# Batch 1 loaded and transposed like batch 0, and GpSimd making the integer addition for w_in's words

## The chip, the cores and the metric

One core of a Trainium2 chip runs the kernel: TensorE (PE, matrix products), VectorE (DVE), ScalarE (ACT), GpSimd (POOL), and SyncE (SP), from whose queue all DMAs of this kernel are issued. The metric is the device time of one execution in microseconds (us), as the median of several runs.

## The reference

Two stages. First, for 8 batches of 8 heads with 576 tokens of 64 dimensions, 32 packed queries p attend to k and v, and the tokens' queries q then attend to the packed result:

```python
def sm_attn(qq, kk, vv):
    s = scale * np.matmul(qq, kk.transpose(0, 1, 3, 2))
    s = s - np.max(s, axis=-1, keepdims=True)
    a = np.exp(s)
    a = a / (np.sum(a, axis=-1, keepdims=True) + 1e-09)
    return np.matmul(a, vv)
p_packed = sm_attn(p, k, v)
out = sm_attn(q, p_packed, p_packed)
```

Its 4608 rows of 512 go through a feed-forward layer with w_in (512 x 2048) and w_out (2048 x 512):

```python
h = x @ w_in
h2 = h * h
h3 = h2 * h
P = a[0] + a[1] * h + a[2] * h2 + a[3] * h3
Q = 1.0 + np.abs(b[0]) * np.abs(h) + np.abs(b[1]) * h2
g = P / (Q + 1e-06)
return (g @ w_out).astype(np.float32)
```

w_in and w_out come in as float64, 8.4 MB each, and the kernel makes float32 of them itself.

## The kernel before, in words

**Units.** The work is cut into 128 units: 8 batches, 2 halves x of 288 tokens, 8 chunks c of 256 hidden columns. `hidden` computes a unit's h in PSUM and the rational function (tiles U, V, Y), and splits the result into a high and a low part, gh and gl. `acc_block` multiplies these by w_out's parts (wh, wl) three units later and accumulates in `acc`. The last 64 tokens of each batch are kept in G and treated two batches at a time by `remainder`.

**Folding.** h is not x @ w_in: `m_chunk(bb, c)` forms M from the packed values (PPT) and w_in, in the PSUM banks `at`, and `hidden` multiplies M by the weights of the second attention, which `attention(bb)` leaves transposed in AH and AL (high and low part).

**Attention.** `attention(bb)` is a generator of 16 steps, laid between the units of the batch before; batch 1's steps lie among batch 0's units. Its steps: k transposed (`transposed("k", g)`), p transposed, scores and exponentials, their transposes, the product with v, q transposed, the second scores, the second softmax. Batch 0 runs ahead of all units and takes another route than the others:
- Batch 0 (`bb == 0`): k, q and v are loaded in long rows, 512 KB in one DMA; PE transposes k and q block by block into PSUM banks and ACT copies them to KX. The last 64 tokens of k and q are loaded apart into a tile r (in a buffer of Y), and transposed by PE as well. The keys lie in parts of 256 and 320, each with a maximum of its own, and a few small DVE operations join the two.
- Batches 1 to 7 (`bb > 0`): k and q are loaded in 144 KB pieces of 128-byte rows so that DVE's 32x32 transpose brings them straight from `nat` into KX; the keys lie in two halves of 288 with a common maximum.

`bank(bb)` gives batch 0 the banks of both `acc` and `at`, and later batches those of `at` alone (2 banks).

**Conversion of the words.** `load_words` brings raw float64 words into buffers that are free at that time (those of m, w, o); `convert` makes float32 of one chunk: two ACT operations (the high word rescaled, the low word's top bits to an integer di), a DVE mask for the sign, a DVE shift-and-or, and the integer addition of hi and di. For w_in (8 chunks, kind "in") the addition writes `win`; for w_out (kind "out") it is followed by a split into high and low part by ACT and POOL. The 17 conversions run from before the first unit into the tenth.

**Order.** All operations are recorded first. `Planner` then ranks them by its own table of costs per engine and writes out the order on every engine, the DMAs on SP's queue too; tiles that share a buffer (`Ring`) follow one another in the order of the program. Each engine works through its list in order. Since every call goes out through one helper, all instructions carry line L216 in the profile, and tiles tell them apart.

Of the kernel before, what the change touches and what calls it, by code (L numbers as in the profile page):

```python
# [13 lines left out]
F32 = mybir.dt.float32  # L14
# [9 lines left out]
P = 128  # L24
# [223 lines left out]
def attention_rational_ffn(  # L248
# [140 lines left out]
    def convert():  # L389
        nonlocal converted  # L390
        if converted == len(words):
            return
        load_words(AHEAD)
        (kind, i, n), raw = words[converted], words_in[converted][1]
        x = 4 if kind == "in" else n
        w = raw.bitcast(I32).rearrange("p (x y two) -> p x y two", x=x, two=2)
        lo, hi = w[:, :, :, 0], w[:, :, :, 1]

        if kind == "in":
            dst = win[:, i // 2]  # L400
            di = dst.bitcast(I32)
        else:
            dst = lo.bitcast(F32)
            di = w_ring.at(i // 2, [P, n * DM], I32) if n == 2 else full_ring.next(dtype=I32)
            di = di.rearrange("p (x y) -> p x y", x=n)
        nc.scalar.activation(hi.bitcast(F32), hi.bitcast(F32), AF.Copy, scale=REBIAS)

        nc.scalar.activation(di, lo.bitcast(U32), AF.Copy, scale=2.0**-29)
        nc.vector.tensor_scalar(lo, hi, -0x80000000, None, ALU.bitwise_and)
        nc.vector.scalar_tensor_tensor(hi, hi, 3, lo, ALU.logical_shift_left, ALU.bitwise_or)  # L410
        nc.vector.tensor_add(dst.bitcast(I32), hi, di)
        if kind == "out":
            if i // 2 not in W:
                W[i // 2] = w_ring.at(i // 2)
            for y in range(n):
                split(dst[:, y, :], *(W[i // 2][:, (i + y) % 2, x, :] for x in range(2)))
        converted += 1
        load_words(AHEAD)
# [6 lines left out]

    NAT, AH, AL, PPT = {}, {}, {}, {}

    def load(bb, what):  # L430
        if bb >= B:
            return
        if what == "rem":

            rv, pn = NAT[bb, "rv"], NAT[bb, "p"] = rv_ring.next(), pn_ring.next()
            if bb == 0:
                r = NAT[bb, "r"] = Y_ring.at(2, [P, H, D])
                nc.sync.dma_start(r[0:REM], k[bb, :, NS * P : T, :].rearrange("h p d -> p h d"))
            for j in range(NJ):
                src = p[bb, NG * j : NG * j + NG].rearrange("r n d -> n r d")  # L440
                nc.sync.dma_start(pn[32 * j : 32 * j + 32, :, 0, :], src)
            nc.gpsimd.tensor_copy(pn[:, :, 1, :], pn[:, :, 0, :])
            for i in range(2 if bb == 0 else 0):
                src = q[bb, 4 * i : 4 * i + 4, NS * P : T, :].rearrange("h (p x) d -> p h (x d)", x=2)
                r2 = r[REM + HREM * i : REM + HREM * (i + 1)].rearrange("p (h x) d -> p h (x d)", x=2)
                nc.sync.dma_start(r2, src)
            for i in range(2):
                src = v[bb, 4 * i : 4 * i + 4, NS * P : T, :]
                if bb == 0:
                    nc.sync.dma_start(rv[REM * i : REM * (i + 1)], src.rearrange("h p d -> p h d"))  # L450
                    continue
                for y in range(2):
                    o = REM * i + HREM * y
                    nc.sync.dma_start(rv[o : o + HREM], src.rearrange("h (p y) d -> y p h d", y=2)[y])
            return
        x, g = what[0], int(what[1])
        src = {"k": k, "q": q, "v": v}[x][bb, 4 * g : 4 * g + 4]
        if bb > 0:
            t = NAT[bb, what] = nat_ring.next()
            if x == "v":  # L460
                t = NAT[bb, what] = t[:, 0 : 4 * NS * D].rearrange("p (h s d) -> p h s d", h=4, s=NS)
                for y in range(2):
                    to = t.rearrange("p h (y i) d -> p h y (i d)", y=2)[:, :, y]
                    nc.sync.dma_start(to, src[:, 2 * P * y : 2 * P * (y + 1)].rearrange("h (p i) d -> p h (i d)", i=2))
                return
            src = src.rearrange("h t d -> (h t) d")
            for i in range(2):
                for y in range(2):
                    o = 64 * i + 32 * y
                    blocks = src[:, 32 * y : 32 * y + 32].rearrange("(a t i) d -> i t a d", t=32, i=2)[i]  # L470
                    nc.sync.dma_start(t[o : o + 32].rearrange("p (a d) -> p a d", d=32), blocks)
            return
        src = src[:, 0 : NS * P, :]
        if x != "k":
            if g == 0:
                NAT[x] = w_ring.at(NCH - 2 + "vq".index(x), [P, 2, 4 * NS * D], F32)
            t = NAT[x][:, g, :]
        else:
            t = nat_ring.next()[:, 0 : 4 * NS * D]
        t = t.rearrange("p (h s d) -> p h s d", h=4, s=NS)  # L480
        nc.sync.dma_start(t, src.rearrange("h (p s) d -> p h s d", s=NS))
        NAT[bb, what] = t
# [18 lines left out]
    def attention(bb):  # L501
# [7 lines left out]
        xr = lambda x: x.rearrange("p (x r) -> p x r", r=NG)  # L509
        eng = nc.vector if bb == 0 else nc.gpsimd  # L510
        KX = kx_ring.next()
        AH[bb], AL[bb], PPT[bb] = AH_ring.next(), AL_ring.next(), ppT_ring.next()
        flat = KX.rearrange("p j c -> p (j c)")
        rows = lambda i: slice(64 * i, 64 * i + 64)
        cols = lambda j: slice(32 * j, 32 * j + 32)
# [4 lines left out]
        qx = flat.rearrange("p (r j c) -> p r j c", r=NG, j=NJ)  # L520

        def transposed(x, g):
            for r in range(NG if bb > 0 else 0):

                src = NAT[bb, f"{x}{g}"].rearrange("p (j r c) -> p r j c", j=2, r=NG)[:, r]
                nc.vector.transpose(qx[:, r, 2 * g : 2 * g + 2, :], src)
            for r in range(NG if bb == 0 else 0):
                t = bank(bb)
                for i in range(2):
                    for y in range(2):  # L530
                        o = (2 * i + y) * P
                        nc.tensor.transpose(t[:, o : o + P], NAT[bb, f"{x}{g}"][:, 2 * i + r, 2 * y : 2 * y + 2, :], ident)
                to = kmain if x == "k" else qx[:, :, :, 0:HMAIN]
                nc.scalar.copy(to[:, r, 2 * g : 2 * g + 2, :], t.rearrange("p (j c) -> p j c", j=2))
# [4 lines left out]
                load(bb, f"v{g}")  # L539
            yield  # L540
        rkq = NAT.get((bb, "r"))
        if bb == 0:
            t = bank(bb)
            for j in range(NJ):
                nc.tensor.transpose(t[:, j * P : (j + 1) * P], rkq[:, 2 * j : 2 * j + 2, :], ident)
            nc.scalar.copy(krem, t.rearrange("p (j c) -> p j c", j=NJ)[:, :, 0:REM])
# [3 lines left out]
        nc.scalar.copy(pT, t[:, 0 : NG * P].rearrange("p (r c) -> p r c", r=NG))  # L550
        yield

        KEYS = ((0, 2 * P), (2 * P, T)) if bb == 0 else ((0, HALF), (HALF, T))
        of = lambda a, r: a.rearrange("p (x r) -> p x r", r=NG)[:, :, r]
        for r in range(NG):
            t = [bank(bb)[:, 0 : c1 - c0] for c0, c1 in KEYS]
            if bb > 0:

                for b in (slice(0, 2 * P), slice(2 * P, HALF)):
                    tiles(  # L560
# [36 lines left out]
                nc.scalar.activation(KX[:, r, c0:c1], t[x], AF.Exp, bias=nb[:, i], scale=SCALE, accum_out=sm[:, i])  # L597
            if r == 0:
                yield
        if bb == 0:  # L600
            nc.vector.tensor_tensor(nbm, nb[:, 0:2], nb[:, 2:4], ALU.min)
            nc.vector.tensor_sub(xr(f), two(nbm), xr(nb))
            nc.scalar.activation(f, f, AF.Exp)
# [2 lines left out]
            fs = sm  # L606
        nc.vector.scalar_tensor_tensor(tot, fs[:, 0:2], 1e-9, fs[:, 2:4], ALU.add, ALU.add)
        nc.vector.reciprocal(rec, tot)
        if bb == 0:
            nc.vector.tensor_mul(xr(F), xr(f), two(rec))  # L610
        yield

        for r in range(NG):
            t = bank(bb)
            for s in range(NS):
                c0 = s * P + (REM if bb > 0 and s > 1 else 0)
                nc.tensor.transpose(t[:, s * P : (s + 1) * P], KX[:, r, c0 : c0 + P], ident)
            nc.scalar.copy(KX[:, 2 + r, 0 : NS * P], t)
            if r == 1:

                t = bank(bb)
                for i in range(NG):
                    o = slice(i * P, (i + 1) * P)
                    if bb > 0:
                        nc.tensor.transpose(t[:, o], KX[:, i, HALF + HREM - P : HALF + HREM], ident)
                        nc.tensor.transpose(t[0:REM, o], KX[:, i, 2 * P : 2 * P + REM], ident)
                        continue
# [4 lines left out]

        t = bank(bb)
        rv = NAT[bb, "rv"]
        for r in range(NG if bb > 0 else 0):
            tiles(
                (
                    (
# [10 lines left out]
                for s in range(NS + 1)  # L649
                for j in range(NJ)  # L650
            )
        for r in range(NG if bb == 0 else 0):
            for x, blocks in enumerate((range(2), range(2, NS + 1))):
                o = slice((2 * r + x) * D, (2 * r + x + 1) * D)
                tiles(
# [19 lines left out]
        twice = lambda o: o.rearrange("p (i d) -> p i d", i=1).broadcast_to([P, 2, D])  # L675
        for r in range(NG):
            o = pp[:, r]
            if bb > 0:
                nc.vector.tensor_scalar(o, twice(t[:, r * D : (r + 1) * D]), rec[:, r : r + 1], None, ALU.mult)
            else:  # L680
                nc.vector.tensor_scalar(o, twice(t[:, 2 * r * D : (2 * r + 1) * D]), F[:, r : r + 1], None, ALU.mult)
# [6 lines left out]
        for g in range(2):  # L688
            transposed("q", g)
            load(bb + 1, f"k{g}")  # L690
            if g == 0 and bb == 0:
                t = bank(bb)
                for j in range(NJ):
                    nc.tensor.transpose(t[:, j * P : (j + 1) * P], rkq[:, 2 * j : 2 * j + 2, :], ident)
# [4 lines left out]
                load(bb + 1, "rem")  # L699
            yield  # L700

        for r in range(NG):
            t = [bank(bb)[:, 0:HALF] for _ in range(2)]
            tiles(
# [135 lines left out]
    def acc_block(u, i):  # L840
# [10 lines left out]
        if i == 0:  # L851
            O[bb, x] = o_ring.next()
        o = O[bb, x]
        order = "(p i x) m -> p x i m" if bb == 0 else "(i p x) m -> p x i m"
        ov = out[bb * T : bb * T + NS * P, :].rearrange(order, i=2, x=2)[:, x]
        if u == NU - 1 and i == 1:
            nc.vector.tensor_copy(o[:, i, :], acc)
# [95 lines left out]
```

## Time and profile before

| | us |
|---|---|
| median of 3 runs (808.62 to 809.86) | 809.83 |
| the profiled execution | 808.45 |
| its span, first to last instruction | 806.7 |
| PE busy in the span | 745.5 (92%) |
| DVE busy | 709.1 (88%) |
| ACT busy | 666.0 (83%) |
| POOL busy | 463.9 (58%) |

The mean granted clock of PE was 0.958. Busy time is an average over the start (attention of batch 0, conversion of the words, batch 0's units with batch 1's attention) and the long rest, where units follow one another evenly; the stages have to be read apart. Times of PE are modelled from pipelined operations. In the rows an operation is named by its engine, its form, and out<-in by tile.

### The profile page before, as it was taken

The numbers are of one execution on the slowest core, as the hardware profiler recorded it, in microseconds if no ns is written. First come the engines' busy times: TensorE is split into PE (matmuls) and PEld (weight loads), VectorE is DVE, ScalarE is ACT, GpSimd is POOL, SyncE is SP. The second block draws the span as 40 slices with busy tenths as digits, with TensorE's granted clock in tenths as the row PEclk, the third lists the DMA queues.
The fourth block names the chain that finished last, engine by engine and source line by source line (L and its number), as shares of the span: only waits on it lengthen the run. The fifth ranks groups of instructions, "written<-read, shape, count | busy, mean of one in ns | idle before, by whom it ended". The sixth has DMA issues, their size and how long they took to land.

```text
span 806.7 us, 15198 instructions
## 1 busy us (share of the span) xinstructions
PE 745.5 (92%) x5416; PEld 585.4 (73%) x5416; DVE 709.1 (88%) x1310; ACT 666.0 (83%) x1482; POOL 463.9 (58%) x462
## 2 busy tenths in 40 slices
PE   6376686899999999999999999999999999999997
PEld 4154464578877788768878788678877887778886
DVE  2988999898899788998899789998899789998873
ACT  4788797799888798889888798889888788998972
POOL 0003564675568455766578555756568456766663
PEclk9765799799999999999999999999999999999999
DMA  8993238202550206220730209120820214000001
GB/s 267 280 298 110 105 78 110 43 5 79 67 86 1 79 18 96 56 57 28 94 58 1 82 15 119 33 56 27 103 49 5 75 33 67 1 2 27 27 1 39
DMA packets 168876, 56.04 MB, mean 69 GB/s; under 512 B 140384, under 2 KB 158048, under 8 KB 168800
## 3 DMA queue, kind: packets, MB, share of 16 engines
q1 hardware_dynamic: 168800, 55.07, 31.4%
q8 instruction: 42, 0.69, 0.4%
q14 instruction: 34, 0.28, 0.1%
HBM read 45.62 MB, written 9.44 MB: 68 GB/s over the span
## 4 chain that ended last, share of the span: by engine, by line
PE 70%; DVE 10%; ACT 8%; SPq 4%; DMA 4%; issue 2%; POOL 1%; DVEq 0%; POOLq 0%
PE acc L216 35%; PE h L216 22%; PE at L216 13%; DVE Y L216 5%; SPq L216 4%; ACT Y L216 2%; DVE w L216 1%; ACT U L216 1%; ACT V L216 1%; ACT w L216 1%; DMA w<-in_q_dram 1%; ACT sq L216 1%; DVE V L216 1%; POOL w L216 1%; DVE kx L216 1%
## 5 line engine op out<-in xcount | busy, mean ns | idle before, releaser
L216 PE MATMUL acc<-w,gh 128*128 128x512 f32 x1024 | 330.5, 405 | 19.3 <-ACT w L216 15.0
L216 PEld LDWEIGHTS acc<-w,gh 128*128 128x128 f32 x1024 | 186.7, 191 | 72.7 <-ACT w L216 16.6
L216 POOL TENSOR_TENSOR U<-U,sq 128x576 f32<-128x576 f32 x118 | 168.9, 1432 | 75.4 <-ACT U L216 43.3
L216 PE MATMUL h<-AH,m 128*128 128x288 f32 x1024 | 192.0, 309 | 8.8 <-DVE Y L216 6.1
L216 POOL TENSOR_TENSOR gl<-Y,gh 128x512 fp32r<-128x512 f32 x128 | 167.7, 1310 | 50.5 <-ACT gh L216 23.3
L216 PE MATMUL acc<-w,gl 128*128 128x512 f32 x512 | 193.2, 398 | 0.3 <-POOL gl L216 0.3
L216 PEld LDWEIGHTS h<-AH,m 128*128 128x128 f32 x1024 | 162.7, 195 | 40.5 <-DVE Y L216 23.1
L216 ACT ACTIVATE Y<-h,abS 128x288 f32<-128x288 f32 x256 | 125.2, 509 | 23.5 <-PE h L216 19.3
L216 DVE TENSOR_TENSOR Y<-Y,h 128x288 f32<-128x288 f32 x256 | 109.9, 446 | 32.0 <-ACT Y L216 12.0
L216 ACT ACTIVATE sq<-h 128x288 f32<-128x288 f32 x236 | 97.5, 416 | 40.2 <-PE h L216 34.1
L216 DVE SCALAR_TENSOR_TENSOR Y<-Y,abS,h 128x288 f32<-128x288 f32 x256 | 125.5, 508 | 2.2
L216 DVE SCALAR_TENSOR_TENSOR Y<-Y,abS,V 128x576 f32<-128x576 f32 x128 | 103.4, 808 | 22.7 <-ACT V L216 22.0
L216 PEld LDWEIGHTS acc<-w,gl 128*128 128x128 f32 x512 | 96.8, 189 | 28.0 <-issue 8.5
L216 PE MATMUL h<-AL,m 128*128 128x288 f32 x512 | 113.0, 302 | 0.0
L216 POOL COPY G<-Y 128x64 f32<-128x64 f32 x128 | 35.5, 277 | 125.8 <-DVE Y L216 109.1
L216 ACT ACTIVATE U<-h 128x288 f32<-128x288 f32 x256 | 98.1, 421 | 8.7 <-PE h L216 4.3
L216 ACT ACTIVATE V<-U,one 128x576 f32<-128x576 f32 x128 | 98.0, 766 | 5.8 <-DVE Y L216 5.6
L216 DVE SCALAR_TENSOR_TENSOR Y<-V,Y 128x576 f32<-128x576 f32 x128 | 95.8, 749 | 1.8
L216 DVE SCALAR_TENSOR_TENSOR V<-U,V 128x576 f32<-128x576 f32 x128 | 96.4, 753 | 0.0
L216 ACT CAST gh<-Y 128x512 fp32r<-128x512 f32 x128 | 81.2, 634 | 7.4 <-DVE Y L216 7.0
L216 PEld LDWEIGHTS h<-AL,m 128*128 128x128 f32 x512 | 85.1, 194 | 0.9 <-issue 0.8
L216 ACT ACTIVATE V<-V 128x576 f32<-128x576 f32 x128 | 84.6, 661 | 0.6
(123 smaller groups left out, 813.2 us busy)
## 6 DMA issues: line engine op xcount, KB each, us to landing
nat<-in_k_dram SPq DMA_DIRECT2D x56, 144.0 KB, 4.1
nat<-in_q_dram SPq DMA_DIRECT2D x56, 144.0 KB, 4.2
out_dram<-o SPq DMA_DIRECT2D x15, 512.0 KB, 2.9
w<-in_moe_w_out_dram SPq DMA_DIRECT2D x14, 512.0 KB, 5.0
nat<-in_v_dram SPq DMA_DIRECT2D x28, 256.0 KB, 3.6
m<-in_moe_w_in_dram SPq DMA_DIRECT2D x8, 512.0 KB, 9.6
w<-in_moe_w_in_dram SPq DMA_DIRECT2D x8, 512.0 KB, 5.5
nat<-in_k_dram SPq DMA_DIRECT2D x2, 512.0 KB, 4.8
```

Source lines behind the costliest of these rows:

```text
L216: getattr(getattr(self.nc, engine), name)(*args, **kwargs)
```

## The change

- In `convert`, the integer addition for w_in's words is made by GpSimd instead of VectorE. For w_out it stays on VectorE.
- `rows4(bb)` is true for batches 0 and 1 and takes the place of `bb == 0` in `load`, `attention` and `acc_block`: batch 1 is loaded, transposed, scored and written out in batch 0's way. It keeps the banks of `at` alone, its softmax stays on GpSimd, and its v and q go into `nat` buffers.
- The tile r of the remainders lies in a buffer of AH (the batch's own), no longer in one of Y; AH and AL of a batch are therefore taken later, after q's transposes, and by the batch's parity.

```diff
-        nc.vector.tensor_add(dst.bitcast(I32), hi, di)
+        eng = nc.gpsimd if kind == "in" else nc.vector
+        eng.tensor_add(dst.bitcast(I32), hi, di)
...
+    rows4 = lambda bb: bb < 2
...
-            if bb == 0:
-                r = NAT[bb, "r"] = Y_ring.at(2, [P, H, D])
+            if rows4(bb):
+                r = NAT[bb, "r"] = AH_ring.at(bb, [P, H, D], F32)
...
-            for i in range(2 if bb == 0 else 0):
+            for i in range(2 if rows4(bb) else 0):
...
-                if bb == 0:
+                if rows4(bb):
                     nc.sync.dma_start(rv[REM * i : REM * (i + 1)], src.rearrange("h p d -> p h d"))
...
-        if bb > 0:
+        if not rows4(bb):
             t = NAT[bb, what] = nat_ring.next()
...
-        if x != "k":
+        if bb == 0 and x != "k":
...
-        AH[bb], AL[bb], PPT[bb] = AH_ring.next(), AL_ring.next(), ppT_ring.next()
+        PPT[bb] = ppT_ring.next()
...
-            for r in range(NG if bb > 0 else 0):
+            for r in range(0 if rows4(bb) else NG):
                 src = NAT[bb, f"{x}{g}"].rearrange("p (j r c) -> p r j c", j=2, r=NG)[:, r]
                 nc.vector.transpose(qx[:, r, 2 * g : 2 * g + 2, :], src)
-            for r in range(NG if bb == 0 else 0):
+            for r in range(NG if rows4(bb) else 0):
                 t = bank(bb)
...
-        KEYS = ((0, 2 * P), (2 * P, T)) if bb == 0 else ((0, HALF), (HALF, T))
+        KEYS = ((0, 2 * P), (2 * P, T)) if rows4(bb) else ((0, HALF), (HALF, T))
...
+        AH[bb], AL[bb] = AH_ring.at(bb % 2), AL_ring.at(bb % 2)
...
-        order = "(p i x) m -> p x i m" if bb == 0 else "(i p x) m -> p x i m"
+        order = "(p i x) m -> p x i m" if rows4(bb) else "(i p x) m -> p x i m"
```

The other places where `bb == 0` or `bb > 0` chose between the two routes in `attention` are changed in the same way.

More of the change, by code (lines that the diff above doesn't have):

```diff
@@ L541, in attention @@
         rkq = NAT.get((bb, "r"))
-        if bb == 0:
+        if rows4(bb):
             t = bank(bb)
@@ L556, in attention @@
             t = [bank(bb)[:, 0 : c1 - c0] for c0, c1 in KEYS]
-            if bb > 0:
+            if not rows4(bb):
                 for b in (slice(0, 2 * P), slice(2 * P, HALF)):
@@ L599, in attention @@
                 yield
-        if bb == 0:
+        if rows4(bb):
             nc.vector.tensor_tensor(nbm, nb[:, 0:2], nb[:, 2:4], ALU.min)
@@ L608, in attention @@
         nc.vector.reciprocal(rec, tot)
-        if bb == 0:
+        if rows4(bb):
             nc.vector.tensor_mul(xr(F), xr(f), two(rec))
@@ L615, in attention @@
             for s in range(NS):
-                c0 = s * P + (REM if bb > 0 and s > 1 else 0)
+                c0 = s * P + (0 if rows4(bb) or s < 2 else REM)
                 nc.tensor.transpose(t[:, s * P : (s + 1) * P], KX[:, r, c0 : c0 + P], ident)
@@ L623, in attention @@
                     o = slice(i * P, (i + 1) * P)
-                    if bb > 0:
+                    if not rows4(bb):
                         nc.tensor.transpose(t[:, o], KX[:, i, HALF + HREM - P : HALF + HREM], ident)
@@ L634, in attention @@
         rv = NAT[bb, "rv"]
-        for r in range(NG if bb > 0 else 0):
+        for r in range(0 if rows4(bb) else NG):
             tiles(
@@ L651, in attention @@
             )
-        for r in range(NG if bb == 0 else 0):
+        for r in range(NG if rows4(bb) else 0):
             for x, blocks in enumerate((range(2), range(2, NS + 1))):
@@ L677, in attention @@
             o = pp[:, r]
-            if bb > 0:
+            if not rows4(bb):
                 nc.vector.tensor_scalar(o, twice(t[:, r * D : (r + 1) * D]), rec[:, r : r + 1], None, ALU.mult)
@@ L690, in attention @@
             load(bb + 1, f"k{g}")
-            if g == 0 and bb == 0:
+            if g == 0 and rows4(bb):
                 t = bank(bb)
```

## The prediction

> **What bounds the kernel now.** First the busy shares of PE and DVE and the row of 40 slices (a digit is the busy tenths of about 20 us), then the busy time by stage.
>
> ```profile
> PE 745.5 (92%) x5416; PEld 585.4 (73%) x5416; DVE 709.1 (88%) x1310; ACT 666.0 (83%) x1482; POOL 463.9 (58%) x462
> ...
> PE   6376686899999999999999999999999999999997
> ...
> DVE  2988999898899788998899789998899789998873
> ```
>
> PE is at 9 from the ninth slice on. Before that PE has gaps (3, 7, 6, 6, 8), and DVE stands at 8 and 9 from the second slice. The whole-span averages, 92% and 88%, therefore mix two stages, and two windows part them:
>
> ```profile
> core 0: us, PE busy (x) PEld busy (x) DVE busy (x) ACT busy (x) POOL busy (x), PEclk, DMA share, GB/s
> 20.00:160.00 140.00, 97.73 (x677) 67.53 (x676) 130.20 (x213) 113.16 (x218) 54.65 (x46) 0.76 0.58 148
> 160.00:806.00 646.00, 635.65 (x4565) 508.54 (x4564) 573.31 (x1072) 543.87 (x1243) 408.24 (x410) 1.00 0.24 46
> ```
>
> The columns are the stretch and its length, then the busy us (and instructions) of PE, PE's weight loads, DVE, ACT, POOL, the clock granted to PE (0.76 and 1.00), the DMA share and GB/s. From 160 us to the end PE is busy 635.65 of 646 us. What is saved on another engine there is worth nearly nothing, since only 10.35 us of PE idle time exist. From 20 to 160 us DVE is busy 130.20 of 140 us, ACT 113.16, PE 97.73, POOL 54.65. The start is a DVE stage with 9.8 us of slack on DVE, 26.8 on ACT, 42.3 on PE and 85 on POOL. Everything this change touches lies in the start: the conversion of w_in, and batch 1's attention, which runs while batch 0's units run. What the start gets shorter, the end comes earlier, because PE's remaining work then begins earlier at full load.
>
> **The change, part by part.**
>
> *GpSimd's adds: taken off DVE.* The integer addition is the custom DVE operation that writes win:
>
> ```profile
> L216 DVE CUSTOM_DVE_ANT_0 win<-m,win 128x2048 uint16<-128x2048 uint16 x4 | 4.9, 1226 | 0.0
> L216 DVE CUSTOM_DVE_ANT_0 win<-w,win 128x2048 uint16<-128x2048 uint16 x4 | 4.9, 1216 | 0.0
> ```
>
> That is 8 adds, 4.9 + 4.9 = 9.8 us of DVE, all before 94 us.
>
> *GpSimd's adds: put on POOL.* POOL has no such add in this trace; its two-input operations on the same 128 rows are nearest:
>
> ```profile
> L216 POOL TENSOR_TENSOR U<-U,sq 128x576 f32<-128x576 f32 x118 | 168.9, 1432 | 75.4 <-ACT U L216 43.3 <-ACT sq L216 15.8 <-DVE Y L216 9.2
> L216 POOL TENSOR_TENSOR gl<-Y,gh 128x512 fp32r<-128x512 f32 x128 | 167.7, 1310 | 50.5 <-ACT gh L216 23.3 <-issue 15.4 <-POOL G L216 6.9
> ...
> L216 POOL TENSOR_TENSOR w<-w,w 128x512 fp32r<-128x512 f32 x14 | 19.6, 1415 | 16.2 <-ACT w L216 10.5 <-issue 5.7
> ```
>
> From 512 to 576 elements the mean rises by 122 ns, 1.91 ns an element; carried on to 1024 elements it is 1310 + 512 x 1.91 = 2.29 us. The lower end is DVE's own 1.22 us; the upper end is the conversion's row, 1415 ns for 512 elements (it has waits in it), doubled: 2.83 us. I take 2.29, as the straight line through undisturbed rows. Eight are 18.3 us. POOL's slack of 85 us holds them, so by busy time they cost nothing. If that cover were gone, the price would be 18.3 us against 9.8 saved. The chunk of w_in comes 1.1 us later to the PE operation that needs it, and SP, whose queue waits for the same addition before it loads the next words into that buffer, waits as much longer:
>
> ```profile
> SPq L216 <- DVE win L216: 12.6, 2, 7.4
> ```
>
> Two such waits, so some 2 us of SP's queue; only DMAs that are already late behind DVE stand behind them, and I cost them at nothing. Behind the add on POOL stand gl, G and the low halves of w_out; each would come up to 2.29 us later, and PE's accumulation waits for gl and w. PE has 42.3 us of slack here, which covers that.
>
> *GpSimd's adds: what they do to DVE.* DVE and POOL stand in each other's way for some operations. Three DVE rows, and the three POOL rows that run beside them:
>
> ```profile
> 76.58 0.51 DVE L216 SCALAR_TENSOR_TENSOR Y<-Y,abS,h 128x288 f32<-128x288 f32 x1
> 87.74 2.36 DVE L216 SCALAR_TENSOR_TENSOR w<-w 128x1024 int32<-128x1024 int32 x2
> 103.43 2.10 DVE L216 CUSTOM_DVE_ANT_0 w<-w,w 128x2048 uint16<-128x2048 uint16 x1
> ```
>
> ```profile
> 76.58 1.28 POOL L216 TENSOR_TENSOR gl<-Y,gh 128x512 fp32r<-128x512 f32 x1 [0.16 <-ACT gh L216]
> 87.17 3.02 POOL L216 COPY G<-Y 128x64 f32<-128x64 f32 x1
> 103.14 1.31 POOL L216 TENSOR_TENSOR w<-w,w 128x512 fp32r<-128x512 f32 x1
> ```
>
> At 103.43 the custom add (1.22 us when alone) takes 2.10: POOL's subtraction began at 103.14 and ran to 104.45, and the add ends 1.1 us after that. At 87.17 POOL's copy of 64 columns takes 3.02 us and ends with DVE's two int32 operations, at 90.1. But at 76.58 a DVE operation that reads h out of PSUM takes its usual 0.51 us beside gl. So DVE operations whose two tensors are both in SBUF exclude POOL's, and the per-unit ones, with one operand in PSUM, do not. Each moved add can therefore stop DVE's next two-SBUF operation, for between 0 and 2.29 us: 0 to 18.3 us in all. To choose, I walk through the eight adds. Each starts when DVE's shift-and-or (the last step before it) is done and runs 2.29 us; what is DVE's next two-SBUF operation then? For four of the eight it is over 2.3 us away. The other four:
>
> ```profile
> 31.42 1.17 DVE L216 SCALAR_TENSOR_TENSOR m<-m 128x1024 int32<-128x1024 int32 x1
> ...
> 33.15 0.76 DVE L216 TENSOR_TENSOR kx<-kx,small 128x576 f32<-128x576 f32 x1
> ...
> 36.48 1.22 DVE L216 SCALAR_TENSOR_TENSOR m<-m 128x1024 int32<-128x1024 int32 x1
> ...
> 38.30 0.73 DVE L216 TENSOR_TENSOR AL<-kx,AH 128x576 fp32r<-128x576 f32 x1
> ...
> 66.78 2.34 DVE L216 SCALAR_TENSOR_TENSOR w<-w 128x1024 int32<-128x1024 int32 x2
> ...
> 69.87 1.47 DVE L216 CUSTOM_DVE_ANT_0 w<-w,w 128x2048 uint16<-128x2048 uint16 x1
> ...
> 90.73 1.78 DVE L216 CUSTOM_DVE_ANT_0 w<-w,w 128x2048 uint16<-128x2048 uint16 x1
> ```
>
> Second chunk: shift-and-or ends at 32.59, the add would run to 34.9, batch 0's subtraction stands at 33.15: 1.7 us. Third: 37.70 to 40.0, AL at 38.30: 1.7. Seventh: 69.12 to 71.4, the custom w add at 69.87: 1.5. Eighth: 90.10 to 92.4, the custom w add at 90.73: 1.7. Together 6.6 us, so the moved adds are worth 9.8 - 6.6 = 3.2 us of DVE, not 9.8.
>
> No row shows waits like the first two of these, because POOL idles 46.61 us through batch 0's attention:
>
> ```profile
> 52.91 0.92 POOL L216 COPY pn<-pn 128x128 f32<-128x128 f32 x1 [46.61 <-DMA pn<-in_p_dram]
> ```
>
> I count them all the same, since batch 0's subtraction and AL's read two tiles of SBUF like the operations that did wait.
>
> The Trainium skill, "SBUF — State Buffer", section "Who interferes with whom", has the port pair as an exclusive lock: a DVE operation with two SBUF inputs and a GpSimd operation that reads SBUF block each other for a whole instruction. By it those two waits, 3.4 us, stay in the sum; without it, with only the conversion's own operations waiting, the sum would be 3.4 us better.
>
> *Batch 1's transposes: taken off DVE.* From 20 to 165 us DVE transposes batch 1's k and q straight from the loaded tile:
>
> ```profile
> L216 DVE STREAM_TRANSPOSE kx<-nat x8: 728/768/784, 42.5 to 137.7; 128x576 f32<-128x576 f32 x8
> ```
>
> 8 x 0.768 = 6.1 us. Against it batch 1 now takes batch 0's route with two key parts of separate maxima, which adds DVE work at these prices:
>
> ```profile
> L216 DVE SCALAR_TENSOR_TENSOR small<-acc,small 128x128 f32<-128x128 f32 x2 | 0.7, 350 | 0.1
> ...
> L216 DVE TENSOR_TENSOR small<-small 128x4 f32<-128x4 f32 x3 | 0.5, 164 | 0.2
> ...
> L216 DVE TENSOR_TENSOR small<-small 128x2 f32<-128x2 f32 x1 | 0.2, 161 | 0.0
> ```
>
> Two of 350 ns, three of 164, one of 161: 1.35 us. Net 4.8 us off DVE. The maxima, biases and normalisations stay equal in number.
>
> *Batch 1's transposes: put on ACT.* PSUM has to be emptied by ACT:
>
> ```profile
> L216 ACT COPY kx<-at 128x512 f32<-128x512 f32 x18 | 10.4, 598 | 1.2 <-PE at L216 1.2
> ...
> L216 ACT COPY kx<-at 128x128 f32<-128x128 f32 x2 | 0.5, 306 | 0.0
> ...
> L216 ACT COPY kx<-at 128x256 f32<-128x256 f32 x1 | 0.4, 372 | 0.3 <-PE at L216 0.3
> ...
> L216 ACT ACTIVATE small<-small 128x4 f32<-128x4 f32 x1 | 0.2, 236 | 0.0
> ```
>
> Eight copies of 128x512, one 128x256 for the remainder's keys, two 128x128 for the remainder's queries, one exponential of 128x4: 4.78 + 0.37 + 0.61 + 0.24 = 6.0 us. ACT's slack is 26.8 us of 140, and a start that is some 8 us shorter leaves 12.8 of it after these 6.0. ACT stands on DVE's way often (it feeds Y, U and V), so I put a quarter, 1.5 us, on the path; the ends are 0 and 6.0.
>
> *Batch 1's transposes: put on PE.* 32 transposes for k and q, 4 and 4 for the remainders:
>
> ```profile
> L216 PE MATMUL at<-ident,kx 128*128 128x128 f32 x76 | 12.6, 274 | 0.0
> ...
> L216 PE MATMUL at<-ident,nat 128*128 128x128 f32 x8 | 2.1, 421 | 0.0
> ```
>
> 40 x 0.274 = 11.0 us at full clock, 40 x 0.421 = 16.8 at the slow one. PE's 42.3 us of slack covers them, at nothing; without it 11.0 would count. They do go through the two at banks, in which batch 1's banks follow one another with the chunks of M in program order:
>
> ```profile
> 20.00:160.00 140.00, 27.60 (x368) 12.12 (x368) 6.51 (x14) 18.06 (x50) 0.76 0.58 148
> ```
>
> PE writes at for 27.6 us and ACT reads it for 18.06 of 140; with 11 and 5.8 more the two banks, 280 us of bank time, are far from full. An order that holds a chunk of M behind a k that has not landed is the risk; I cost it at 0 and keep the end of one landing, 4.8 us.
>
> *Batch 1's DMAs.* 28 issues become 15: k and q go from 16 to 4, v from 4 to 2, the v remainder from 4 to 2, p stays at 4, and 3 are new (the remainders of k and q, into AH's second buffer, which is idle until batch 1's own AH).
>
> ```profile
> nat<-in_k_dram SPq DMA_DIRECT2D x56, 144.0 KB, 4.1
> ...
> nat<-in_k_dram SPq DMA_DIRECT2D x2, 512.0 KB, 4.8
> ```
>
> Four issues of 144 KB, each 4.1 us to landing, become one of 512 KB with 4.8. The eight q issues hold SP 6.71 us:
>
> ```profile
> 117.10 6.71 SPq L216 DMA_DIRECT2D nat<-in_q_dram  x8
> ```
>
> Two of these would take a quarter of that, 1.7 us, and q's transposes can start some 5 us sooner. DVE is full at that time whatever lands, so this makes room for the order and is no term. Batch 0's remainder moves from a Y buffer to an AH buffer; both are empty then, so nothing. The late choice of AH is nothing for later batches, which alternate as before.
>
> **The sum.** DVE: -9.8 + 6.6 - 4.8 = -8.0; ACT on the path +1.5: -6.5 us. The profiled execution took 808.45 us (span 806.7, 1.75 around it), so it becomes 802.0. The median of the runs, 809.83, lies 1.4 above that execution: 803.4 is the forecast. The order of all instructions is planned anew, which can move the 10.35 us of PE idle time after 160 us by some 2 either way.
>
> **The rivals.**
>
> *POOL's adds stop DVE (slower).* If the new order puts a two-SBUF operation of DVE right behind every shift-and-or, as the conversion of w_out's words does at 87.74 and 90.73, all eight waits are whole: 18.3 instead of 6.6 us. Then -9.8 + 18.3 - 4.8 + 1.5 = +5.2, 815.0 us. It decides from a mean wait of (9.8 + 4.8 - 1.5) / 8 = 1.6 us an add; the walk gave 6.6 / 8 = 0.8, and for it speaks that four of eight already have such a neighbour, against it that the units' own DVE work lies between conversions. Chance 0.13. The Trainium skill's "GPSIMD Engine Reference", section "Engine selection", speaks for this side: elementwise two-input work belongs on VectorE, GpSimd being about twice as slow; the rows' 2.29 against 1.22 agree.
>
> *ACT takes over.* The whole 6.0 us comes onto the path: -8.0 + 6.0 = -2.0, 807.8 us. For it: ACT is at 81% of the stage and would reach 90% of 132 us; against it: DVE would still be at 93%. Chance 0.14, half of it no change.
>
> *The gain does not arrive.* A chunk of M behind k's banks, or the wait of PE for w_out's words, gives the time back before 160 us: 809.8. Against it: DVE is the late one in those waits. Chance 0.08.
>
> *All of it arrives.* No wait behind POOL and ACT hidden: -9.8 - 4.8 = -14.6, 795.2 us. For it: the plan may put non-excluding unit work behind each addition. Chance 0.20.
>
> **How the numbers follow.** The forecast has 0.45. No change is what lies within 0.2%, 1.6 us, about what a measurement of this kernel can tell. Faster: 0.45 + 0.20 + 0.07 = 0.72; same: 0.07 + 0.08 = 0.15; slower 0.13. The range runs from 796, near all of it arriving, to 811, which takes in no change and leaves out most of the slower case. The faster cases alone span 795 to 808.
>
> **What would show it.** In the profile after: eight POOL additions into win of about 2.3 us; no DVE transpose from nat before 165 us except later batches'; DVE's busy time some 8 us below 709.1; the ninth-slice 9 of PE reached some 6 us earlier, and the stage after it as long as before. Wrong: the shift, AL or custom operations of DVE lengthened by over 1.6 us an add; POOL's add far from 2.3 us; PE idle in the start with at as its reason; or PE's idle time after 160 us changed by more than 2 us.

## The result: 0.7% faster, 804.53 us

The changed kernel takes 804.53 us (median of 4 runs, 803.05 to 805.15) against 809.7 us for the kernel before: a ratio of 0.9932, with a 95% interval of 0.9918 to 0.9946. That is 5.2 us less; the forecast was 6.4 less, within 796 to 811.

The page of the changed kernel first, busy shares and slices:

```profile
PE 746.0 (93%) x5440; PEld 586.8 (73%) x5440; DVE 706.3 (88%) x1300; ACT 671.2 (84%) x1494; POOL 484.8 (60%) x470
...
PE   6478598799999999999999999999999999999997
...
DVE  2899999989899789998899789998899789998883
```

PE again stands at 9 from the ninth slice on. The two stages (columns as named in the first row; the two numbers after POOL are the granted clock and the DMA share):

```profile
core 0: us, PE busy (x) PEld busy (x) DVE busy (x) ACT busy (x) POOL busy (x), PEclk, DMA share, GB/s
20.00:160.00 140.00, 100.19 (x726) 70.71 (x725) 133.99 (x222) 119.25 (x238) 79.23 (x58) 0.80 0.47 148
160.00:803.00 643.00, 632.76 (x4541) 506.63 (x4539) 567.58 (x1062) 541.05 (x1235) 404.60 (x406) 1.00 0.26 47
```

After 160 us PE is busy 632.76 of 643 us, so 10.24 us are idle, against 10.35 before: the long stage is as it was. In the start DVE is now busy 133.99 of 140 us instead of 130.20, so DVE is still what is late there, and fuller than before. Over the whole span its busy time fell by 2.8 us, from 709.1 to 706.3.

The moved additions, as GpSimd's operations on win (min, median and max in ns, first and last start in us), and who waited for them:

```profile
L216 POOL TENSOR_TENSOR win<-m,win x4: 2407/2609/2861, 21.7 to 39.9; 128x1024 int32<-128x1024 int32 x4
L216 POOL TENSOR_TENSOR win<-w,win x4: 2410/2624/3313, 46.1 to 85.5; 128x1024 int32<-128x1024 int32 x4
```

```profile
PEld at L216 <- POOL win L216: 8.4, 3, 5.5
...
PE at L216 <- POOL win L216: 7.7, 3, 5.3
```

An undisturbed one takes 2.41 us. The four longer ones (2.81 to 3.31 us) each began 0.5 to 1.1 us before a product, a mask, a subtraction or a shift-and-or of DVE ended. PE waited 7.7 us in all for chunks of win. Before, when DVE made them, it was 6.1 us:

```profile
PE at L216 <- DVE win L216: 6.1, 2, 5.5
```

DVE's rows in the start, and the GpSimd rows beside them:

```profile
31.44 2.24 DVE L216 TENSOR_SCALAR m<-m 128x1024 int32<-128x1024 int32 x1
...
36.26 2.31 DVE L216 TENSOR_TENSOR kx<-kx,small 128x576 f32<-128x576 f32 x1
...
40.53 2.42 DVE L216 TENSOR_TENSOR kx<-kx,small 128x576 f32<-128x576 f32 x1
...
46.60 3.60 DVE L216 TENSOR_SCALAR w<-w 128x1024 int32<-128x1024 int32 x2
...
51.26 0.44 DVE L216 TENSOR_TENSOR Y<-Y,h 128x288 f32<-128x288 f32 x1
...
86.47 2.89 DVE L216 TENSOR_SCALAR w<-w 128x1024 int32<-128x1024 int32 x1
...
105.02 1.00 DVE L216 TENSOR_TENSOR small<-small 128x4 f32<-128x4 f32 x1
```

```profile
30.33 2.81 POOL L216 TENSOR_TENSOR win<-m,win 128x1024 int32<-128x1024 int32 x1 [6.24 <-DVE m L216]
...
35.09 2.86 POOL L216 TENSOR_TENSOR win<-m,win 128x1024 int32<-128x1024 int32 x1 [1.96 <-DMA w<-in_moe_w_out_dram]
...
39.92 2.41 POOL L216 TENSOR_TENSOR win<-m,win 128x1024 int32<-128x1024 int32 x1 [1.97 <-DVE m L216]
...
46.15 2.81 POOL L216 TENSOR_TENSOR win<-w,win 128x1024 int32<-128x1024 int32 x1 [3.82 <-DVE w L216]
...
85.49 3.31 POOL L216 TENSOR_TENSOR win<-w,win 128x1024 int32<-128x1024 int32 x1 [1.16 <-DVE w L216]
...
103.38 2.61 POOL L216 TENSOR_TENSOR w<-w,w 128x512 fp32r<-128x512 f32 x2
```

Read them in pairs. GpSimd's add at 30.33 ends at 33.14, and DVE's mask, begun at 31.44, ends 0.5 us later and takes 2.24 us instead of 0.69. The product of batch 0's softmax at 36.26 ends 0.6 us after the add of 35.09; the one at 40.53 ends 0.6 us after the add of 39.92; the masks at 46.60 stand behind the add of 46.15, and the mask at 86.47 behind that of 85.49. With 0.69 for a mask (1.30 for two in a row) and 0.74 for a product as the undisturbed times these five wait 1.55, 1.6, 1.7, 2.3 and 2.2 us, 9.3 us in all. Three of the five waits are at masks, which read one tensor only. Four of the five stand ahead of unit 0, whose first DVE operation comes at 51.26, where it came at 45.33 before; and still the kernel ends earlier. The rows of before, with its unit 0 and a pair of masks:

```profile
45.33 0.45 DVE L216 TENSOR_TENSOR Y<-Y,h 128x288 f32<-128x288 f32 x1 [1.41 <-ACT U L216]
...
48.89 1.30 DVE L216 TENSOR_SCALAR w<-w 128x1024 int32<-128x1024 int32 x2
```

The same in groups, first of the kernel before and then of the changed one (count | busy us, mean ns):

```profile
L216 DVE SCALAR_TENSOR_TENSOR w<-w 128x1024 int32<-128x1024 int32 x11 | 13.7, 1259 | 0.0
...
L216 DVE TENSOR_SCALAR w<-w 128x1024 int32<-128x1024 int32 x11 | 8.1, 763 | 1.2 <-ACT w L216 1.2
...
L216 DVE TENSOR_TENSOR kx<-kx,small 128x576 f32<-128x576 f32 x4 | 3.0, 738 | 0.0
...
L216 DVE TENSOR_SCALAR m<-m 128x1024 int32<-128x1024 int32 x4 | 2.8, 696 | 1.1 <-ACT win L216 1.1
```

```profile
L216 DVE SCALAR_TENSOR_TENSOR w<-w 128x1024 int32<-128x1024 int32 x11 | 14.8, 1356 | 0.0
...
L216 DVE TENSOR_SCALAR w<-w 128x1024 int32<-128x1024 int32 x11 | 12.2, 1118 | 0.8 <-ACT w L216 0.7
...
L216 DVE TENSOR_TENSOR kx<-kx,small 128x576 f32<-128x576 f32 x4 | 6.2, 1550 | 0.0
...
L216 DVE TENSOR_SCALAR m<-m 128x1024 int32<-128x1024 int32 x4 | 4.2, 1059 | 0.0
```

Masks on w +3.9 us (11 x 355 ns), products +3.2, masks on m +1.5, shift-and-or +1.1: 9.7 us more for the same work, against 9.8 us of additions taken away. On the other side the route of batch 1 is as the diff says:

```profile
L216 ACT COPY kx<-at 128x512 f32<-128x512 f32 x26 | 15.3, 597 | 3.5 <-PE at L216 3.3
...
L216 PE MATMUL at<-ident,nat 128*128 128x128 f32 x40 | 8.8, 362 | 0.3 <-ACT ppT L216 0.3
```

```profile
nat<-in_k_dram SPq DMA_DIRECT2D x4, 512.0 KB, 8.1
...
nat<-in_q_dram SPq DMA_DIRECT2D x2, 512.0 KB, 5.0
```

ACT's copies are 8 more (18 to 26) at the same 597 ns, PE's transposes of nat 32 more at 362 ns, and k's and q's loads take 8.1 and 5.0 us to land, for half a megabyte each.

### The profile page after: what moved, and what is told of

Same layout as the page of the kernel before. It is cut to its first block, busy times and chain, and to the rows that moved or that the text cites. A ratio compares the mean times of both kernels' runs of the same rounds, so it can differ in the third digit from the quotient of the medians.

```text
span 803.3 us, 15260 instructions
## 1 busy us (share of the span) xinstructions
PE 746.0 (93%) x5440; PEld 586.8 (73%) x5440; DVE 706.3 (88%) x1300; ACT 671.2 (84%) x1494; POOL 484.8 (60%) x470
## 4 chain that ended last, share of the span: by engine, by line
PE 72%; DVE 14%; ACT 9%; issue 3%; POOL 1%; DMA 1%; SPq 0%; ACTq 0%; DVEq 0%; POOLq 0%
PE acc L216 37%; PE h L216 22%; PE at L216 13%; DVE Y L216 5%; DVE w L216 3%; ACT Y L216 2%; DVE kx L216 1%; ACT V L216 1%; ACT U L216 1%; DVE m L216 1%; ACT sq L216 1%; ACT w L216 1%; DVE small L216 1%; ACT m L216 1%; ACT kx L216 1%
## 5 line engine op out<-in xcount | busy, mean ns | idle before, releaser
L216 PE MATMUL acc<-w,gh 128*128 128x512 f32 x1024 | 327.1, 401 | 10.9 <-ACT w L216 4.5
L216 PEld LDWEIGHTS acc<-w,gh 128*128 128x128 f32 x1024 | 184.1, 189 | 62.8 <-ACT gh L216 9.4
L216 POOL COPY G<-Y 128x64 f32<-128x64 f32 x128 | 32.5, 254 | 109.0 <-DVE Y L216 98.0
## 6 DMA issues: line engine op xcount, KB each, us to landing
w<-in_moe_w_in_dram SPq DMA_DIRECT2D x8, 512.0 KB, 10.7
```

What stands on the lines that cost most here:

```text
L216: getattr(getattr(self.nc, engine), name)(*args, **kwargs)
```

## The experiments

Theory 1 says that the start is DVE's, that batch 1's route takes DVE work away, and that GpSimd's adds give back in port waits (DVE standing still behind a GpSimd operation) what they save. Its rivals: the adds carry their half of the gain; the start is bound elsewhere; the loads carry it.

**Each part alone.** The first keeps batch 1's new route and leaves the addition on VectorE; the second is the kernel before with the adds moved.

```diff
-        eng = nc.gpsimd if kind == "in" else nc.vector
+        eng = nc.vector
```

> Only batch 1's route is changed; the addition of w_in's words stays on DVE. Theory 1 (ports): in the changed kernel the eight adds save 9.8 us of DVE, but DVE's two-SBUF operations wait some 9.3 us behind them, so the adds are worth 0.5 us and the route carries the gain: about 804 to 805 us, no slower than with both parts. Theory 2 (each half its share): without the adds half the gain is gone, 807 us.

Measured: 804.09 us, ratio 0.9927 (0.9911 to 0.9943). The route alone gives what both parts give together.

```diff
-        nc.vector.tensor_add(dst.bitcast(I32), hi, di)
+        eng = nc.gpsimd if kind == "in" else nc.vector
+        eng.tensor_add(dst.bitcast(I32), hi, di)
```

> Only the eight adds go to GpSimd; batch 1 keeps its route. Theory 1 (ports): 9.8 saved, about as much lost in waits: 809 to 811 us, within 0.2% of the kernel before. Theory 2 (each half its share): 807 us.

Measured: 806.19 us, 0.9956 (0.9941 to 0.9972). Here theory 1 misses: the adds alone do gain 0.44%. But any change of the work also makes the planner write a new order, so the two causes have to be parted. The next kernels plan with one engine and issue to the other, and so keep every other instruction in its place.

**The engine of the adds, at a fixed order.** At issue, after planning, the eight operations go to the other engine, or are left out:

```diff
             for name, args, kwargs in calls:
+                if engine == "gpsimd" and name == "tensor_add" and args[0].dtype == I32:
+                    engine = "vector"
                 getattr(getattr(self.nc, engine), name)(*args, **kwargs)
```

In the changed kernel's order, on DVE:

> The changed kernel in its own order, only the eight additions issued to DVE at the place in that order where GpSimd had them. Theory 1: DVE gets 9.8 us back and loses 9.3 us of waits: 804 to 806 us. Rival (the adds on GpSimd do relieve DVE): 809 to 813 us.

Measured: 802.07 us, 0.9907 (0.9890 to 0.9925). Theory 1 wanted about the changed kernel's time; this is faster than its range. In the start DVE now has:

```profile
20.00:160.00 140.00, 97.74 (x735) 70.98 (x736) 134.86 (x231) 120.61 (x239) 60.46 (x53) 0.85 0.48 149
```

In the order planned for the adds alone, on DVE:

> The order of instructions planned for the adds alone on GpSimd (806.2 us), but the eight additions issued to DVE at their places in it. Theory 1 (new order): what the adds alone gained comes from the order that the planner wrote for a lighter DVE, and GpSimd itself costs some 2 us, as it did in the changed kernel's order: 802 to 805 us. Theory 2 (GpSimd relieves DVE): the 9.8 us come back to DVE, 808 to 812 us.

Measured: 803.41 us, 0.9919 (0.9904 to 0.9934), against 0.9956 (0.9941 to 0.9972) with GpSimd in the same order. In the order of the kernel before, on GpSimd (the same edit from vector to gpsimd, for win alone):

> The order of the kernel before, the eight additions issued to GpSimd at their places in it. Theory 1 (ports): DVE saves 9.8 us and waits for at least the 6.6 us of the prediction's walk, and the chunks come later to PE: 808 to 813 us, no gain. Theory 2 (GpSimd relieves DVE): 804 to 807 us.

Measured: 809.74 us, 1.0000 (0.9990 to 1.0011). Together, each as a ratio to runs of the kernel before beside it:

| order planned for | adds on DVE | adds on GpSimd |
|---|---|---|
| the kernel before | 1 | 1.0000 |
| the adds alone moved | 0.9919 | 0.9956 |
| both parts | 0.9907 | 0.9932 |

Read along a row, GpSimd never helps: it costs nothing, 0.37% and 0.25% (the last pair's intervals, 0.9890 to 0.9925 and 0.9918 to 0.9946, overlap a little, and those of the pair above do not). Read down the column of DVE, the order planned for the moved adds gains 0.8% with no work changed at all. So what the adds alone gained was their order.

The traces show DVE getting little time back from GpSimd and PE waiting longer. From left to right in the three rows of the table, DVE's busy time over the whole span goes from 709.1 to 707.3, from 709.6 to 710.1 and from 706.1 to 706.3 us, while PE's waits for a chunk of win go from 6.1 to 7.8, from 2.0 to 5.2 and from 4.5 to 7.7 us. In the old order the 1.8 us that DVE was less busy became idle time: 12.2 us of the start instead of 9.8.

```profile
20.00:160.00 140.00, 97.55 (x674) 68.46 (x673) 127.76 (x204) 112.61 (x217) 74.63 (x54) 0.77 0.58 148
```

The old order with GpSimd shows the waits where the prediction's walk had them, in batch 0's product and in AL (738 and 746 ns before):

```profile
L218 DVE TENSOR_TENSOR kx<-kx,small 128x576 f32<-128x576 f32 x4 | 4.7, 1186 | 0.0
...
L218 DVE TENSOR_TENSOR AL<-kx,AH 128x576 fp32r<-128x576 f32 x2 | 3.3, 1653 | 0.0
```

And the adds left out, in the changed kernel's order:

```diff
+                if engine == "gpsimd" and name == "tensor_add" and args[0].dtype == I32:
+                    continue
```

> The changed kernel in its own order of instructions, with the eight additions left out where they would be issued (w_in's low words are not added, so the values differ). Theory 1: the 9.3 us for which DVE waits behind GpSimd's adds go, DVE is late in the start, so the end comes 5 to 9 us earlier: 796 to 800 us. Rival (the start is bound elsewhere, by ACT or the loads, and the waits lie beside it): within 1.5 us of the changed kernel, 803 to 806 us.

Measured: 797.56 us, 0.9846 (0.9826 to 0.9866), 0.9% below the changed kernel and inside theory 1's range. This takes away three things at once: DVE's 9.3 us of waits, GpSimd's own time, and PE's waits for win; together they are worth 7 us, and the run does not part them. Against the same order with the additions on DVE (802.07 us) it is 4.5 us faster, for 10.4 us of additions (4.8 and 5.6 us in that trace). Without them win keeps what ACT wrote there, the integers from the low words, so PE multiplies other numbers; the clock granted from 20 to 160 us was 0.84, against 0.85 with the additions on DVE and 0.80 in the changed kernel.

**Is the route's gain DVE's time?** DVE is refilled in the kernel with the route alone, in its order:

```diff
                 nc.scalar.copy(to[:, r, 2 * g : 2 * g + 2, :], t.rearrange("p (j c) -> p j c", j=2))
+                if bb == 1:
+                    nc.extra[len(nc.ops) - 1] = [(scratch, win[:, 0, 0, :])] * 2
...
+            for to, src in self.extra.get(i, ()):
+                self.nc.vector.transpose(to, src)
```

> The kernel with batch 1's route alone (804.1 us), in its own order, with sixteen DVE transposes of 128x256 into a scratch tile issued beside ACT's eight copies (2 each, some 5.5 us of DVE, near the 6.1 that the route took away). Theory 1 (DVE's time is the gain): 808 to 810 us. Rival (the gain comes from fewer and longer loads and their order): 804 to 805.5 us.

Measured: 809.91 us, 1.0000 (0.9989 to 1.0011). The whole gain is gone, with the loads, the order and the route as they were, so the loads alone do not carry it. The added operations:

```profile
L219 DVE STREAM_TRANSPOSE scratch<-win x16: 431/440/446, 47.9 to 130.6; 128x256 f32<-128x256 f32 x16
```

Sixteen of 440 ns are 7.0 us; since neighbours overlap a little, DVE's busy time on the page rises by 5.7 us, from 708.4 to 714.1.

And the opposite in the kernel before:

```diff
+                if name == "transpose" and engine == "vector" and args[1].tensor.name.startswith("nat"):
+                    left -= 1
+                    if left >= 0:
+                        self.nc.vector.transpose(*args)
```

> The kernel before in its own order, each of batch 1's eight DVE transposes of k and q issued twice (6.1 us more of DVE). Theory 1 (DVE is late throughout the start): 4 to 6 us slower, 814 to 816 us. Rival (the transposes lie beside other waits): under 2 us slower, up to 812 us.

Measured: 812.73 us, 1.0036 (1.0021 to 1.0051): 2.5 us slower for 6.1 us of work, less than theory 1 wanted. The window shows where the rest went:

```profile
20.00:160.00 140.00, 92.63 (x650) 64.03 (x651) 135.36 (x210) 109.37 (x209) 48.17 (x43) 0.78 0.60 147
```

DVE's idle time in the start fell from 9.8 to 4.6 us. The doubled transposes fill holes that the old order leaves in DVE: the row of DVE's largest wait in the start of the kernel before (who waited for whom: us in total, times, longest):

```profile
DVE Y L216 <- ACT U L216: 5.2, 5, 1.7
```

So a microsecond of DVE costs nearly its full price in the route's order and less than half in the old one, and these two runs do not part the route's own gain. With the route alone DVE's busy time over the whole span is 708.4 us, only 0.7 below the kernel before: the eight transposes are gone, but other operations of DVE, small ones and shift-and-ors, took longer. What fell is DVE's idle time in the start, from 9.8 to 5.7 us:

```profile
PE 745.3 (93%) x5440; PEld 585.8 (73%) x5440; DVE 708.4 (88%) x1308; ACT 670.2 (84%) x1494; POOL 458.9 (57%) x462
...
20.00:160.00 140.00, 103.62 (x740) 72.57 (x741) 134.34 (x226) 120.22 (x240) 53.75 (x50) 0.85 0.48 150
```

How much of the route's gain is work taken off DVE, and how much the order that came with it, stays open.

**Why that order is better.** The order planned for the moved adds, issued with all of them on DVE:

```profile
20.00:160.00 140.00, 98.35 (x713) 70.63 (x721) 136.97 (x229) 116.73 (x229) 56.95 (x50) 0.80 0.58 150
```

DVE is busy 136.97 of 140 us: 3.0 us idle instead of 9.8, for the same work. Its largest wait in that stretch:

```profile
DVE Y L218 <- ACT V L218: 1.4, 2, 1.1
```

The wait of 5.2 us for ACT's U is no longer there. To see whether any new order does this, the kernel before was planned again with no work changed:

```diff
-    PASS = 200
+    PASS = 230
```

> The kernel before with no work changed: only the planner's assumed delay between two engines is 230 ns instead of 200, which gives another order. Theory 3 (in the start a new order alone moves the kernel by several us through DVE's idle time): over 2 us from 810, on either side. Rival (orders are equal to within the measurement): 808.5 to 811.5 us.

Measured: 810.19 us, 1.0003 (0.9994 to 1.0012).

> The same with 170 ns. Theory 3: over 2 us from 810, on either side. Rival: 808.5 to 811.5 us.

Measured: 808.24 us, 0.9979 (0.9968 to 0.9990). So theory 3 falls in this form: a new order as such gives 0 and 0.2%, while the order for the moved adds gave 0.8%.

**A planner that knows the ports.** It treats GpSimd's operations and DVE's port-taking ones as exclusive:

```diff
+                if other and back is None and port[other] > now:
+                    near = [x for x in heapq.nsmallest(6, ready[e]) if not self.port[x[1]]]
...
+                        wait = port[other] - now
...
-                end[i] = free[e] = now + self.costs[i]
+                end[i] = free[e] = now + wait + self.costs[i]
```

> The changed kernel, its planner taught that GpSimd's operations and DVE's two-SBUF or one-source SBUF operations exclude each other. Theory (the port waits are what GpSimd's adds cost): most of the 15.7 us of waits go, 798 to 803 us. Rival (the planner's own guesses matter more than this one): 803 to 807 us.

Measured: 805.19 us, 0.9935 (0.9920 to 0.9951).

> Batch 1's route alone with the adds on DVE, the planner taught the same. Only 5.8 us of waits are there to save: 799 to 804 us. Rival (a new order moves the time either way, whatever it knows): 802 to 808 us.

Measured: 807.19 us, 0.9969 (0.9956 to 0.9982). Both fail. With both parts it is where the changed kernel is, and with the route alone it is slower than without the knowledge (0.9927). The knowledge took away few of the waits: DVE's busy time over the span is 704.1 instead of 706.3 us with both parts, and 707.1 instead of 708.4 with the route alone. So these two runs do not show what an order without the waits would be worth.

## Why the prediction was right, and where its steps were off

**The bound.** "The start is a DVE stage" holds for the route's order, where sixteen operations put on DVE took the gain back whole. In the order of the kernel before it holds only in part: there 1.8 us less of busy DVE gained nothing, and 6.1 us more cost 2.5. The stage after 160 us kept its idle time (10.35 and 10.24 us).

**The added operations' own sizes.** GpSimd's add was put at 2.29 us and takes 2.41 undisturbed; ACT's eight copies came as counted. PE's transposes took 362 ns in the mean of the 40, between the two ends of 274 and 421. That 421 is the time at a slow clock, as the prediction has it, is not shown: the granted clock was 1.00 from 4.9 to 10.7 us, where the kernel before makes its 421 ns transposes.

**DVE's -8.0 us: this term was mis-sized.** DVE's busy time over the span was to fall by some 8 us and fell by 2.8. One part is the port waits. The walk gave four waits and 6.6 us; the trace has five, 9.3 us. For the old order the walk was nearly right: batch 0's products and AL wait 1.8 us each there (4 x 448 and 2 x 907 ns), where it had 1.7. (What it calls a subtraction at 33.15 is a product.) But the walk took DVE's neighbours from the old order. In the new one five additions instead of three start ahead of unit 0, four of them meet a product or a mask, and masks were not in the walk's rule of two SBUF tensors. The rival's deciding point, 1.6 us an add, was not reached: 9.3 / 8 = 1.2. The Trainium skill's rule ("SBUF — State Buffer", "Who interferes with whom"), that a DVE operation with two SBUF inputs is blocked for the whole of a GpSimd operation that reads SBUF, is seen here in batch 0's products (1550 instead of 738 ns), which no row of the trace before could show. Another part is the route's small operations: they came in the number counted, but took 2.7 us more than before instead of 1.35 (the six products and differences of 128x4, 299 ns in the mean instead of 164), since some of them waited too.

**The moved adds' 3.2 us of DVE: this step failed.** At a fixed order they are worth nothing or cost 2 to 3 us. In the old order, where the walk's waits came nearly as sized, DVE was 1.8 us less busy and none of it reached the end. The step costed the later chunks of win at nothing, because PE had slack; at a fixed order PE's waits for them grew by 1.7, 3.2 and 3.2 us. What part of the cost is these waits and what part DVE's is not shown.

**The route.** Net 4.8 us of DVE less 1.5 for ACT, 3.3 us in all, was too little: alone it gave 5.9 us (0.73%). And it did not come by the path that the sum has: DVE's busy time fell by 0.7 us, not 4.8, and the rest is less idle time. Whether a quarter of ACT's copies lies on the path was not tested.

**The order.** The prediction let a new order move PE's idle time after 160 us by some 2 us either way. That was too narrow and in the wrong stage: 6.8 us lay between two orders of the same work, and DVE's idle time in the start went from 9.8 to 3.0 us between them. So the sum came out near 5.2 because an overrated gain of the adds and an underrated gain of the route, both mixed with a new order, cancelled. That the number came so close is luck.

**The rivals.** "ACT takes over" and "the gain does not arrive" did not come; ACT is busy 119.25 of 140 us and DVE 133.99. "POOL's adds stop DVE" is the right mechanism, short of its deciding point.

**Open.** Why the order planned for the moved adds keeps DVE fuller than other orders of the same work is not settled. It is shown that it does (3.0 us idle against 9.8), not what in the planner leads to it; two other assumed delays did not find it, nor did the knowledge of the ports. The kernel with both parts planned and the adds issued to DVE (802.07 us, 0.9907) is the fastest of those with the whole computation. That it beats the changed kernel is likely, not shown, since the intervals overlap.

## What to carry to other kernels

Before moving work from DVE to GpSimd, count which of DVE's remaining operations read two SBUF tensors or are masks like the one here: these stood still while GpSimd worked, and an addition that takes 1.2 us on DVE and 2.4 on GpSimd is then no relief. Where a planner orders the instructions, part "less work" from "another order" by planning one way and issuing the other; here the order alone was worth more than the engine. What a microsecond of the late engine is worth depends on the order too: 7.0 us put on DVE cost 5.8 in one order, 6.1 us cost 2.5 in another, and 10.4 us left out gained 4.5 in a third. One run with a duplicate put back shows it.

## What the runs showed that was not expected

- Tiny operations wait as well: DVE's product on 128x4 at 105.02 took 1.00 us (164 ns in the mean before), while GpSimd's two subtractions ran from 103.38 to 105.99.
- Planning with a wrong engine for eight adds and then issuing them to the old one made the kernel 0.8% faster (803.41 us) with no work changed.
